# Packing the last 96 columns of gate and up into fewer TensorE matmuls, in a scheduled two-block kernel

## The chip, the core and the metric

The kernel runs on one core of one Trainium2 chip. The metric is device time in microseconds (us) of that core, lower is better. "The profile" is a page and a trace of one execution; times in it count from the start of its span, and the span is about 1.7 us shorter than the device time of the same run. Engines are named as in the profile: PE is TensorE (PEld its weight loads), DVE is VectorE, ACT is ScalarE, POOL is GpSimd, SP is the engine whose queue issues nearly all DMAs here.

## The reference, cut to what matters

Four residual layers in a row: linear attention (A), gated ReGLU (B), A, B, with the same weights both times. S is 2048 tokens, D is 512, H is 32 heads of 16, F is 1376. All data are bfloat16.

```python
x = x + A(layernorm(x))   # qkv, softmax feature maps, kv state, normalise, wo
x = x + B(layernorm(x))
x = x + A(layernorm(x))
x = x + B(layernorm(x))

def B(x, W_gate, W_up, W_down):
    gate = x @ W_gate             # [2048, 512] @ [512, 1376]
    up   = x @ W_up
    return (relu(gate) * up) @ W_down
```

The number that matters is 1376 = 10 x 128 + 96. A full matmul of this kernel has 128 columns of weights (its stationary operand) and N tokens (its moving operand, N = 512 in most of them). The last chunk of gate and the last chunk of up each use 96 of the 128 columns.

## The kernel before

Tokens are 16 tiles of 128, or 4 slabs of 512. For each slab and each chunk `fc` of 128 columns, `step` does four matmuls for gate and four for up (D = 512 is four contractions of 128), a relu on ACT and a product on DVE. The sums of a matmul land in a bank of PSUM, from which ACT and DVE read them:

```python
def step(fc):
    Mf = 128 if fc < 10 else FLAST                       # FLAST = 96
    gb, ub = next(ring), next(ring)                      # two PSUM banks
    ...
    for bank, W, wr in ((gb, k.Wg, "Wg"), (ub, k.Wu, "Wu")):
        for ic in range(NC):                             # NC = 4
            op("pe", ... e.matmul(k.pb[bank][0:Mf, 0:n], W[:, ic, fc*128:fc*128+Mf],
                                  k.yT[:, ic, c0:c0+n], start=(ic == 0), stop=(ic == NC-1)),
               [r(wr, ic)] + RY, [self.RP[bank]], du, ...)
    op("act", ... relu: gate_sb <- pb[gb] ..., 170 + n * 0.833, ...)
    ...                                                  # product on DVE into hT[u]
for fc in range(NFC):                                    # NFC = 11
    out.append(lambda fc=fc: step(fc))
```

The kernel is not written in its final order. Every instruction is recorded as an `op` with what it reads, what it writes, its engine and a fixed duration. At build time a list scheduler works out ranks from the end of the program backwards, simulates it forwards, tries 48 variants of the ranks, and keeps the order with the shortest makespan (the modelled time to the last end, averaged over 6 replays with slightly varied durations). This order of each engine is then what runs.

```python
def _forward(self, prio):
    ...
        nxt[e] = min([(max(free[e], t), prio[i], i) for i, t in avail[e].items() if place[i] < lim], default=None)
    ...
        free[o.eng] = st + o.dur            # an engine is held for the op's fixed duration
        if o.is_dma:
            q_free = max(st + self.DMA_FIXED * 0.35, q_free) + o.dma_bytes / self.DMA_BW
            finish[i] = q_free + self.DMA_FIXED * 0.65
```

The first layer norm applies its scale and shift, mostly on DVE, and each tile is then transposed by a DMA on SP's queue. The late weights (8 pieces of `wo`, gate, up, down) are loaded on the same queue. In the model an ordinary DMA holds SP for 450 ns, a transpose for 1190 ns; a DVE instruction takes the same time whatever GpSimd does.

```python
# ln(): tiles 4 to 15 of the first layer norm
op(how, ... e.tensor_scalar(k.ytile[:, yb, :], k.x_sb[:, t, :], k.rstd[:, t, :], k.nmr[:, t, :], ...),
   dep, dst, 407 if how == "dve" else 2090, f"{tag} apply {t}")
self.dma_tr(... k.yT[:, :, t*128:(t+1)*128] <- k.ytile[:, yb, :] ..., f"{tag} tr {t}")      # "L0 tr 14" below

# late_weights(): on SP as well
dma("sp", ... k.wo_p[h:128:8, :, :] <- wo_v[h] ..., 65536, f"dma wo{h}")                    # h = 0..7
dma("sp", ... W[:, c, :] <- src[c*128:(c+1)*128, :] ..., 128 * F * 2, f"dma {nm}{c}")       # Wg, Wu
```

The softmax here doesn't subtract the row's maximum and nothing guards it: scores larger than these inputs give would overflow.

Of the kernel before, what the change touches and what calls it, by code (L numbers as in the profile page):

```python
# [368 lines left out]
class Kernel:  # L369
# [27 lines left out]
    def alloc(self, E):  # L397
        nc = self.nc

        def sb(name, shape, dt=BF16):  # L400
            t = E(nc.sbuf_tensor(name, [P] + shape, dt))
            setattr(self, name, t)
            return t

        sb("x_sb", [NT, 512])
        sb("yT", [NC, S])
        sb("wv_p", [NC, 512])
        sb("Wqp", [NC, 512])
        sb("Wkp", [NC, 512])
        sb("wo_p", [NC, 512])  # L410
        sb("Wg", [NC, F])
        sb("Wu", [NC, F])
        sb("Wd", [NFC, 512])
        sb("expk", [NT, 2, 512])
        sb("vsb", [NT, NC, 130])
        sb("expq", [NSLAB, NC, 2, 512])
        sb("kvbd", [NG, GW])
        sb("hT", [NHU, 512])
        sb("numbf", [2, NG, GW])
        sb("tsc", [2, 1024])  # L420
        sb("osb", [2, 512])
        sb("oT", [4, NC, 128])
        sb("gate_sb", [3, 512])
        sb("ytile", [4, 512])
        sb("ident", [128])
        sb("mask8", [8])
        sb("mask8t", [8])
        sb("phi_c", [NC, DH])
        sb("stats6", [NT, 6], FP32)
        sb("mv", [NT, 2], FP32)  # L430
        sb("rv1", [NT, 1], FP32)
        sb("rstd", [NT, 1], FP32)
        sb("nmr", [NT, 1], FP32)
        sb("agg", [4, 3], FP32)
        sb("aggw", [2], FP32)
        sb("mhalf", [4, 1], FP32)
        sb("Zk", [2, 64], FP32)
        sb("rZk", [4, 64], FP32)
        sb("zm", [2, 64], FP32)
        sb("zd", [2, 32], FP32)  # L440
        sb("zr", [2, 32], FP32)
        sb("ab", [2, 64])
        self.ps = E(nc.psum_tensor("ps", [P, 8, 512], FP32))
        self.pb = [self.ps[:, i, :] for i in range(8)]
        self.RP = [self.r("pb", i) for i in range(8)]


    def setup(self):
# [17 lines left out]
        op("pool", lambda e: e.affine_select(k.mask8t[:], ones_c[:, 0:8], [[-16, 8]], ALU.is_ge, 0.0, base=0, channel_multiplier=1),  # L466
           [r("tsc", 0)], [r("mask8t")], 200, "mask8 a")
        op("pool", lambda e: e.affine_select(k.mask8[:], k.mask8t[:], [[16, 8]], ALU.is_ge, 0.0, base=15, channel_multiplier=-1),
           [r("mask8t")], [r("mask8")], 200, "mask8 b")

        n0 = len(self.prog.ops)

        def ldx(t0, t1, after=()):
            dma("sp", lambda e: e.dma_start(k.x_sb[:, t0:t1, :], xv[:, t0:t1, :]), list(after), [r("x", t) for t in range(t0, t1)], 131072 * (t1 - t0) if t1 > t0 + 1 else 96000, f"dma x{t0}")
        dma("sp", lambda e: e.dma_start(k.phi_c[:], A_w_phi.rearrange("(kc hl) d f -> (hl d) kc f", hl=8)), [], [r("phi_c")], 16384, "dma phi")
        for ic in range(NC):
# [10 lines left out]
        for j, o in enumerate(self.prog.ops[n0:]):  # L487
# [5 lines left out]
            k.mask8[:].unsqueeze(1).unsqueeze(3).to_broadcast([P, NC, 8, DH]), ALU.mult),  # L493
           [r("phi_c"), r("mask8")], [R_BD], 1040, "BD")
        op("pool", lambda e: e.memset(k.aggw[:, 0:1], -0.5), [], [r("aggw")], 100, "agg w0")
# [246 lines left out]

    def glu_up(self, ts, ring, tag, out, on_act=()):
        op, r, k = self.op, self.r, self
# [27 lines left out]

        for fc in range(NFC):
            out.append(lambda fc=fc: step(fc))

    def glu_down(self, t, ring, tag, halves=1):
# [20 lines left out]
    def emit(self):  # L797
        from itertools import cycle
        self.unit, self.unit_of = 0, {}
        self.setup()  # L800
# [28 lines left out]
        for i, piece in enumerate(pieces):  # L829
            piece(self.r("yT", 15 if i < 8 else 15))  # L830
        kv(6, 2)
        kv(8, 2)
# [6 lines left out]
        for li in (0, 2):  # L839
# [10 lines left out]

            def steps_B(ts, on_act=()):
                out = []
                self.glu_up(ts, gring, B, out, on_act)
                for t in ts:
                    out.append(lambda t=t: self.glu_down(t, dring, B, 1 + (last and t == NT - 1)))
                    if last:
                        out.append(lambda t=t: self.store(t, 1 + (t == NT - 1)))
                return out

            def steps_N(ts):  # L860
                return [lambda t=t: N([t]) for t in ts]
# [29 lines left out]
            if not last:  # L891
                mix(steps_B(tiles(2)), steps_N([14, 15]) + steps_K(0))
                mix(steps_B(tiles(3)), steps_K(1) + steps_K(2) + [lambda: self.q_proj(0, mring, "A2")])
                for t in range(12):
                    self.kv_acc(t, "A2")
                for f in steps_K(3):
                    f()
                for t in tiles(3):
                    self.kv_acc(t, "A2")
                self.kv_fin("A2")  # L900
            else:
                mix(steps_B(tiles(2), HA), [])
                mix(steps_B(tiles(3), HA), [])

# [67 lines left out]
```

## Time and profile before

| | before |
|---|---|
| device time, median of 3 runs | 391.91 us (391.82 to 392.07) |
| span of the profiled run | 390.3 us |
| granted TensorE clock | 1.000 |
| PE busy | 379.4 us, 97% |
| start to start of two N=512 matmuls in a full stretch | 0.216 us |

These are the first line of the page of the kernel before (busy time, share of the span, instructions) and the first line of its chain of waits (which engines make up the chain that ended last).

```profile
PE 379.4 (97%) x2331; PEld 208.0 (53%) x2331; DVE 272.0 (70%) x547; ACT 206.6 (53%) x389; POOL 168.5 (43%) x284
PE 88%; POOL 4%; ACT 3%; DMA 2%; DVE 1%; issue 1%; ACTq 0%; POOLq 0%
```

TensorE bounds it. That is not so over the whole length, as the table of busy time by stretch of the same kernel shows (stretch, its length, then PE, PEld, DVE, ACT, POOL busy us with instruction counts, granted clock, DMA share, GB/s):

```profile
0.00:50.00 50.00, 44.15 (x311) 24.96 (x311) 44.43 (x70) 39.81 (x60) 39.87 (x59) 1.00 0.57 153
...
100.00:150.00 50.00, 50.00 (x271) 24.93 (x270) 37.82 (x80) 18.41 (x36) 22.58 (x49) 1.00 0.24 43
```

The two largest PE waits before (who waited, for what: total us, times, longest):

```profile
PE ps L509 <- DMA hT<-in_A_wqkv_dram: 3.6, 2, 3.2
PE ps L617 <- ACT yT L605: 1.0, 1, 1.0
```

The groups by shape of the same kernel show what the change is after (line, engine, operation, out<-in, stationary, moving, count | busy us, mean ns | idle before). A matmul is drawn 379 ns long but its successor starts after 216 ns; these 0.216 us are called a slot below.

```profile
L758 PE MATMUL ps<-yT,Wu 128*96 128x512 bf16 x24 | 9.1, 379 | 0.0
L758 PE MATMUL ps<-yT,Wg 128*96 128x512 bf16 x24 | 8.9, 379 | 0.0
```

There are 24 and 24 of these matmuls, each using 96 of 128 columns (slabs 1 to 3 of both gated layers, four contractions each; the missing slab 0 runs in halves of N=256).

### The profile page before, as it was taken

Reading aid. Unit: us, or ns where it says so; the run is one execution under the profiler, and the core shown is the slowest. Engines: PE = TensorE matmul, PEld = TensorE weight load, DVE = VectorE, ACT = ScalarE, POOL = GpSimd, SP = SyncE. Lnnn points to the kernel's source line nnn. Section 1 sums busy time; section 2 is a strip of 40 time slices with the busy share of each in tenths; the row PEclk is TensorE's granted clock in tenths of the full one; section 3 lists DMA queues with packets and bytes.
Section 4 is the critical chain, followed back from the end, with each engine's and each line's share of the span. In section 5 each row is a group of like instructions: output and inputs, shape, how many; then the busy total and the mean of one; then the engine's idle time right before and its main releaser. Section 6 shows DMA issues by size and latency. Waiting matters only on the chain.

```text
span 390.3 us, 6397 instructions
## 1 busy us (share of the span) xinstructions
PE 379.4 (97%) x2331; PEld 208.0 (53%) x2331; DVE 272.0 (70%) x547; ACT 206.6 (53%) x389; POOL 168.5 (43%) x284
## 2 busy tenths in 40 slices
PE   5999989999999999999999999999999999999997
PEld 3445554667644544444444457567774554444444
DVE  4999978877766888866766777897986776232222
ACT  5898859834633404533453484985563462553340
POOL 5499936641724363372244543584553242100000
DMA  6833682311311322401000110132323132100002
GB/s 179 228 67 71 191 299 53 69 40 32 53 40 27 43 55 44 84 10 28 14 15 0 27 29 3 40 80 57 55 55 69 27 42 67 29 14 27 17 12 67
DMA packets 61663, 23.01 MB, mean 59 GB/s; under 512 B 53472, under 2 KB 60608, under 8 KB 61632
## 3 DMA queue, kind: packets, MB, share of 16 engines
q1 hardware_dynamic: 60912, 22.02, 24.4%
q10 hardware_dynamic: 720, 0.59, 0.5%
q8 instruction: 18, 0.29, 0.3%
q14 instruction: 13, 0.11, 0.1%
HBM read 7.91 MB, written 2.10 MB: 26 GB/s over the span
## 4 chain that ended last, share of the span: by engine, by line
PE 88%; POOL 4%; ACT 3%; DMA 2%; DVE 1%; issue 1%; ACTq 0%; POOLq 0%
PE ps L758 39%; PE ps L785 19%; PE ps L617 7%; PE ps L737 7%; PE ps L690 6%; PE ps L706 4%; PE ps L663 3%; PE ps L648 2%; POOL expk L634 2%; ACT expq L693 2%; DVE stats L551 1%; DMA x_sb<-in_A_x_dram 1%; DMA hT<-in_A_wqkv_dram 1%; ACT expk L620 1%; POOL rstd L576 1%
## 5 line engine op out<-in xcount | busy, mean ns | idle before, releaser
L758 PE MATMUL ps<-yT,Wg 128*128 128x512 bf16 (+3 forms) x440 | 130.1, 337 | 0.5 <-DMA yT<-ytile 0.2
L758 PE MATMUL ps<-yT,Wu 128*128 128x512 bf16 (+3 forms) x440 | 129.6, 336 | 0.0
L760 ACT ACTIVATE gate_sb<-ps 128x512 bf16<-128x512 f32 (+3 forms) x110 | 55.9, 512 | 105.3 <-PE ps L758 102.9
L785 PE MATMUL ps<-Wd,hT 128*128 128x512 bf16 (+2 forms) x363 | 106.8, 373 | 0.0
L634 POOL TENSOR_TENSOR expk<-expk,rZk 128x1024 bf16<-128x1024 bf16 (+1 forms) x32 | 59.5, 1878 | 37.1 <-DVE rZk L631 19.7
L758 PEld LDWEIGHTS ps<-yT,Wg 128*128 128x128 bf16 (+1 forms) x440 | 43.4, 100 | 33.8 <-issue 1.1
L758 PEld LDWEIGHTS ps<-yT,Wu 128*128 128x128 bf16 (+1 forms) x440 | 43.7, 100 | 32.6 <-ACT expk L765 0.2
L767 DVE TENSOR_TENSOR hT<-gate_sb,expk 128x512 bf16<-128x512 bf16 (+3 forms) x73 | 29.8, 409 | 37.9 <-ACT expk L765 33.0
L785 PEld LDWEIGHTS ps<-Wd,hT 128*128 128x128 bf16 (+1 forms) x363 | 35.3, 98 | 36.6 <-DVE x_sb L787 0.6
L551 DVE BATCH_NORM_STATS2 stats<-x_sb 128x6 f32<-128x512 bf16 x64 | 42.6, 682 | 5.5 <-DMA x_sb<-in_A_x_dram 5.1
L366 ACT ACTIVATE numbf<-ps 128x432 bf16<-128x432 f32 x64 | 33.1, 536 | 19.5 <-PE ps L706 19.4
L629 DVE TENSOR_REDUCE Zk<-expk 128x64 f32<-128x1024 bf16 x32 | 37.7, 1194 | 5.7 <-ACT expk L620 5.4
L731 POOL TENSOR_TENSOR osb<-tsc 128x512 bf16<-128x512 bf16 x28 | 32.5, 1162 | 19.9 <-DVE tsc L726 17.8
L737 PE MATMUL ps<-wo_p,oT 128*128 128x512 bf16 x128 | 39.8, 379 | 0.0
L770 DVE TENSOR_TENSOR hT<-gate_sb,ps 128x512 bf16<-128x512 bf16 (+2 forms) x37 | 22.7, 613 | 20.8 <-PE ps L758 19.6
L693 ACT ACTIVATE expq<-ps 128x1024 bf16<-128x1024 f32 (+1 forms) x40 | 32.6, 861 | 7.3 <-PE ps L690 7.0
L765 ACT ACTIVATE expk<-ps 128x512 bf16<-128x512 f32 (+3 forms) x73 | 36.1, 497 | 0.1
L706 PE MATMUL ps<-kvbd,expq 128*128 128x144 bf16 x256 | 35.0, 226 | 0.5 <-ACT numbf L366 0.5
L620 ACT ACTIVATE expk<-ps 128x512 bf16<-128x512 f32 x44 | 23.9, 598 | 21.5 <-PE ps L617 21.2
L690 PE MATMUL ps<-yT,Wqp 128*128 128x512 bf16 x128 | 34.6, 379 | 0.6 <-ACT expq L693 0.5
L787 DVE TENSOR_TENSOR x_sb<-x_sb,ps 128x512 bf16<-128x512 bf16 (+1 forms) x33 | 22.0, 669 | 18.8 <-PE ps L785 18.4
L559 POOL TENSOR_TENSOR rstd<-rv,mhalf 128x1 f32<-128x1 f32 (+1 forms) x53 | 31.9, 607 | 2.9
(73 smaller groups left out, 429.2 us busy)
## 6 DMA issues: line engine op xcount, KB each, us to landing
out_dram<-x_sb SPq DMA_DIRECT2D x15, 128.0 KB, 1.7
x_sb<-in_A_x_dram SPq DMA_DIRECT2D x3, 512.0 KB, 6.2
Wu<-in_B_W_up_dram SPq DMA_DIRECT2D x4, 344.0 KB, 5.9
Wg<-in_B_W_gate_dram SPq DMA_DIRECT2D x4, 344.0 KB, 5.5
Wd<-in_B_W_down_dram SPq DMA_DIRECT2D x5, 256.0 KB, 6.9
yT<-ytile SPq DMA_TRANSPOSE x60, 2.5
hT<-in_A_wqkv_dram ACTq DMA_DIRECT2D x4, 128.0 KB, 3.1
x_sb<-in_A_x_dram SPq DMA_DIRECT2D x4, 128.0 KB, 3.7
```

The source lines that it names most:

```text
L366: return e.activation(out, in_, ACT.Copy) if hasattr(e, "activation") else e.tensor_copy(out, in_)
L551: op("dve", (lambda t: lambda e: e.bn_stats(k.stats6[:, t, :], k.x_sb[:, t, :]))(t), [r("x", t)], [r("st", t)], 685, f"{tag} stats {t}")
L629: op("dve", lambda e: e.tensor_reduce(k.Zk[:, zb, :], k.expk[:, t, :, :].rearrange("p s (h f) -> p (s h) f", f=16), AX.X, ALU.add), [r("ex ...
L634: op(eng, (lambda s0, s1: lambda e: e.tensor_tensor(k.expk[:, t, s0:s1, :].rearrange("p s (h f) -> p (s h) f", f=16), k.expk[:, t, s0:s1, ...
L690: op("pe", (lambda c, ic, bank: lambda e: e.matmul(k.pb[bank][:], k.Wqp[:, ic, c * 128:(c + 1) * 128], k.yT[:, ic, st * 512:(st + 1) * 512 ...
L693: op("act", (lambda c0, s, b0: lambda e: e.activation(k.expq[:, st, c0:c0 + w, s, :], k.ps[:, b0:b0 + w, :], ACT.Exp, scale=(1.0 - 2.0 * s ...
L706: op("pe", (lambda s, c, j, g0, bank: lambda e: e.matmul(k.pb[bank][:, j * GW:(j + 1) * GW], k.expq[:, st, c, s, tt * 128:(tt + 1) * 128], ...
L737: op("pe", (lambda c, bank: lambda e: e.matmul(k.pb[bank][:], k.oT[:, ob, c, :], k.wo_p[:, c, :], start=(c == 0), stop=(c == NC - 1)))(c, ...
L758: op("pe", (lambda bank, W, ic, fc, Mf: lambda e: e.matmul(k.pb[bank][0:Mf, 0:n], W[:, ic, fc * 128:fc * 128 + Mf], k.yT[:, ic, c0:c0 + n] ...
L760: op("act", (lambda Mf, gb, gs: lambda e: e.activation(k.gate_sb[0:Mf, gs, 0:n], k.pb[gb][0:Mf, 0:n], ACT.Relu))(Mf, gb, gs), [self.RP[gb] ...
L765: op("act", (lambda Mf, ub, tu: lambda e: e.activation(k.expk[0:Mf, tu, 0, 0:n], k.pb[ub][0:Mf, 0:n], ACT.Copy))(Mf, ub, tu), [self.RP[ub] ...
L785: op("pe", (lambda fc, Kf, u, c0, bank, m0, m1: lambda e: e.matmul(k.pb[bank][:, m0:m1], k.hT[0:Kf, u, c0:c0 + 128], k.Wd[0:Kf, fc, m0:m1] ...
```

## The change

In the last two slabs of each gated layer the remaining 96 columns of gate and 96 of up are split. 64 + 64 of them form one full 128-column stationary, one group of four matmuls per slab. The remaining 32 + 32 form a 64-column stationary, which is meant to be used on both halves of the array's columns at once, one half for slab 2 and one for slab 3: eight matmuls that are hoped to take four slots. Per layer, 16 slots for two slabs become 8 + 4. GpSimd copies the columns once into a packed weight tile `Wr`, 192 columns wide. To make room, two small setup tensors move into buffers that are free at that time.

The diff, cut to its core (the rest are the buffer moves and the bookkeeping of which buffer of `hT` belongs to which slab):

```diff
+        sb("Wr", [NC, 192])
-        sb("mask8t", [8])
-        sb("phi_c", [NC, DH])
+        self.mask8t = self.tsc[:, 1, 0:8]
+        self.phi_c = self.hT[:, 13, 0:NC * DH].rearrange("p (c f) -> p c f", c=NC)
...
+    def pack_weights(self):
+        for W, nm, o0, o1 in ((k.Wu, "Wu", 0, 128), (k.Wg, "Wg", 64, 160)):
+            for dst, src, n in ((o0, 1280, 64), (o1, 1344, 32)):
+                op("pool", ... e.tensor_copy(k.Wr[:, :, dst:dst + n], W[:, :, src:src + n]) ..., 200 + 4 * n, f"pack {nm} {dst}")
...
-        for fc in range(NFC):
+        def short64():
+            ...
+            for ic in range(NC):
+                op("pe", ... e.matmul(k.pb[bank][:, 0:n], k.Wr[:, ic, 0:128], k.yT[:, ic, c0:c0 + n], ...), ..., du, ...)
+            op("act", ... relu: gate_sb[0:64] <- pb[bank][64:128] ...)
+            op("dve", ... hT[0:64] <- gate_sb[0:64] * pb[bank][0:64] ...)
+
+        def short32():
+            ...
+            def mm(e):
+                for ic in range(NC):
+                    for v in range(2):
+                        last = e.matmul(k.pb[bank][v * 64:v * 64 + 64, 0:n], k.Wr[:, ic, 128:192], k.yT[:, ic, c0 + v * n:c0 + v * n + n], start=(ic == 0), stop=(ic == NC - 1), skip_group_check=True)
+                return last
+            op("pe", mm, ..., 4 * du + 190, ...)
+            ...                                   # relu and product of 32 partitions, once per slab
+
+        for fc in range(NFC - 1 if short else NFC):
             out.append(lambda fc=fc: step(fc))
+        if short:
+            out.append(short64)
+        if short == 2:
+            out.append(short32)
...
-                mix(steps_B(tiles(2)), steps_N([14, 15]) + steps_K(0))
-                mix(steps_B(tiles(3)), steps_K(1) + steps_K(2) + ...)
+                mix(steps_B(tiles(2), (), 2), steps_N([14, 15]) + steps_K(0))
+                mix(steps_B(tiles(3), (), 1), steps_K(1) + steps_K(2) + ...)
...
-                mix(steps_B(tiles(2), HA), [])
-                mix(steps_B(tiles(3), HA), [])
+                mix(steps_B(tiles(2), HA, 2), [])
+                mix(steps_B(tiles(3), HA, 1), [])
```

The diff fixes no instruction's place in the running order: as before, the scheduler orders everything anew.

More of the change, by code (lines that the diff above doesn't have):

```diff
@@ L466, in setup @@
         op("pool", lambda e: e.affine_select(k.mask8t[:], ones_c[:, 0:8], [[-16, 8]], ALU.is_ge, 0.0, base=0, channel_multiplier=1),
-           [r("tsc", 0)], [r("mask8t")], 200, "mask8 a")
+           [r("tsc", 0)], [r("tsc", 1)], 200, "mask8 a")
         op("pool", lambda e: e.affine_select(k.mask8[:], k.mask8t[:], [[16, 8]], ALU.is_ge, 0.0, base=15, channel_multiplier=-1),
-           [r("mask8t")], [r("mask8")], 200, "mask8 b")
+           [r("tsc", 1)], [r("mask8")], 200, "mask8 b")
         n0 = len(self.prog.ops)
@@ L474, in ldx @@
             dma("sp", lambda e: e.dma_start(k.x_sb[:, t0:t1, :], xv[:, t0:t1, :]), list(after), [r("x", t) for t in range(t0, t1)], 131072 * (t1 - t0) if t1 > t0 + 1 else 96000, f"dma x{t0}")
-        dma("sp", lambda e: e.dma_start(k.phi_c[:], A_w_phi.rearrange("(kc hl) d f -> (hl d) kc f", hl=8)), [], [r("phi_c")], 16384, "dma phi")
+        dma("sp", lambda e: e.dma_start(k.phi_c[:], A_w_phi.rearrange("(kc hl) d f -> (hl d) kc f", hl=8)), [], [r("hT", 13)], 16384, "dma phi")
         for ic in range(NC):
@@ L493, in setup @@
             k.mask8[:].unsqueeze(1).unsqueeze(3).to_broadcast([P, NC, 8, DH]), ALU.mult),
-           [r("phi_c"), r("mask8")], [R_BD], 1040, "BD")
+           [r("hT", 13), r("mask8")], [R_BD], 1040, "BD")
         op("pool", lambda e: e.memset(k.aggw[:, 0:1], -0.5), [], [r("aggw")], 100, "agg w0")
@@ L740, in num, with glu_up @@
            [r("x", t), self.RP[bank]], [r("x", t)], 685, f"{tag} resid {t}")
-    def glu_up(self, ts, ring, tag, out, on_act=()):
+    def pack_weights(self):
+        op, r, k = self.op, self.r, self
+        for W, nm, o0, o1 in ((k.Wu, "Wu", 0, 128), (k.Wg, "Wg", 64, 160)):
+            for dst, src, n in ((o0, 1280, 64), (o1, 1344, 32)):
+                op("pool", (lambda W, dst, src, n: lambda e: e.tensor_copy(k.Wr[:, :, dst:dst + n], W[:, :, src:src + n]))(W, dst, src, n),
+                   [r(nm, ic) for ic in range(NC)], [r("Wr", dst)], 200 + 4 * n, f"pack {nm} {dst}")
+    def glu_up(self, ts, ring, tag, out, on_act=(), short=0):
         op, r, k = self.op, self.r, self
@@ L771, in step @@
                    [r("gate", gs), self.RP[ub]], [r("hT", u)], 150 + n * 1.04, f"{tag} h {ts[0]} {fc}")
-        for fc in range(NFC):
-            out.append(lambda fc=fc: step(fc))
+        def short64():
+            bank = next(ring)
+            u = self.short_of.pop(ts[0], None)
+            if u is None:
+                u = self.new_short(ts)
+            gs = u % 3
+            for ic in range(NC):
+                op("pe", (lambda ic: lambda e: e.matmul(k.pb[bank][:, 0:n], k.Wr[:, ic, 0:128], k.yT[:, ic, c0:c0 + n], start=(ic == 0), stop=(ic == NC - 1)))(ic),
+                   [r("Wr", 0), r("Wr", 64)] + RY, [self.RP[bank]], du, f"{tag} Wr {ts[0]} {ic}")
+            op("act", lambda e: e.activation(k.gate_sb[0:64, gs, 0:n], k.pb[bank][64:128, 0:n], ACT.Relu),
+               [self.RP[bank]], [r("gate", gs)], 170 + n * 0.833, f"{tag} relu {ts[0]} a")
+            op("dve", lambda e: e.tensor_tensor(k.hT[0:64, u, 0:n], k.gate_sb[0:64, gs, 0:n], k.pb[bank][0:64, 0:n], ALU.mult),
+               [r("gate", gs), self.RP[bank]], [r("hT", u)], 150 + n * 1.04, f"{tag} h {ts[0]} a")
@@ new lines, in short32 @@
+        def short32():
+            bank = next(ring)
+            t2 = list(range(ts[-1] + 1, ts[-1] + 1 + len(ts)))
+            us = [self.unit_of[ts[0], NFC - 1][0], self.new_short(t2)]
+            self.short_of[t2[0]] = us[1]
+            def mm(e):
[3 more added lines that the diff above has]
+                return last
+            op("pe", mm, [r("Wr", 128), r("Wr", 160)] + RY + [r("yT", t) for t in t2], [self.RP[bank]], 4 * du + 190, f"{tag} Wr2 {ts[0]}")
+            for v, u in enumerate(us):
+                gs = u % 3
+                op("act", (lambda v, gs: lambda e: e.activation(k.gate_sb[64:96, gs, 0:n], k.pb[bank][v * 64 + 32:v * 64 + 64, 0:n], ACT.Relu))(v, gs),
+                   [self.RP[bank]], [r("gate", gs)], 170 + n * 0.833, f"{tag} relu {ts[0]} b{v}")
+                op("dve", (lambda v, gs, u: lambda e: e.tensor_tensor(k.hT[64:96, u, 0:n], k.gate_sb[64:96, gs, 0:n], k.pb[bank][v * 64:v * 64 + 32, 0:n], ALU.mult))(v, gs, u),
+                   [r("gate", gs), self.RP[bank]], [r("hT", u)], 150 + n * 1.04, f"{tag} h {ts[0]} b{v}")
@@ L776, in glu_down, with new_short @@
+        for fc in range(NFC - 1 if short else NFC):
+            out.append(lambda fc=fc: step(fc))
+        if short:
+            out.append(short64)
+        if short == 2:
+            out.append(short32)
+    def new_short(self, ts):
+        u = self.unit % NHU
+        self.unit += 1
+        for t in ts:
+            self.unit_of[t, NFC - 1] = (u, (t - ts[0]) * 128)
+        return u
     def glu_down(self, t, ring, tag, halves=1):
@@ L798, in emit @@
         from itertools import cycle
-        self.unit, self.unit_of = 0, {}
+        self.unit, self.unit_of, self.short_of = 0, {}, {}
         self.setup()
@@ L830, in emit @@
             piece(self.r("yT", 15 if i < 8 else 15))
+        self.pack_weights()
         kv(6, 2)
@@ L849, in N, with steps_B @@
                     self.ln(t, L1)
-            def steps_B(ts, on_act=()):
+            def steps_B(ts, on_act=(), short=0):
                 out = []
-                self.glu_up(ts, gring, B, out, on_act)
+                self.glu_up(ts, gring, B, out, on_act, short)
                 for t in ts:
@@ L891, in emit @@
             if not last:
-                mix(steps_B(tiles(2)), steps_N([14, 15]) + steps_K(0))
-                mix(steps_B(tiles(3)), steps_K(1) + steps_K(2) + [lambda: self.q_proj(0, mring, "A2")])
+                mix(steps_B(tiles(2), (), 2), steps_N([14, 15]) + steps_K(0))
+                mix(steps_B(tiles(3), (), 1), steps_K(1) + steps_K(2) + [lambda: self.q_proj(0, mring, "A2")])
                 for t in range(12):
```

## The prediction

> **What bounds the kernel now.** TensorE. The page has PE busy for 379.4 of 390.3 us (97%). That figure overstates the matmul work, because a 128x512 matmul is drawn 379 ns long while the timeline shows the next one starting 216 ns later. But the busy-time table by stretch gives 50.00 of 50 us from 100 to 200 us and 49.8 from 200 to 300, and the waits view lists no PE wait over 0.2 us in the gated layers. From about 70 us on, PE starts a matmul every 216 ns (N=512) without a hole. The chain of waits agrees: 88% PE, 39% in the gate/up line. So a 216 ns matmul slot taken away in the gated layers should come off the span almost one for one.
>
> **What the change removes.** The last 96 columns of gate and up take 4+4 matmuls of N=512 per slab. The view by shape lists them: 128x96 stationary, 24 for each weight over slabs 1 to 3 of both layers. In slabs 2 and 3 of a layer that is 16 slots = 16 x 0.216 = 3.46 us. After: two packed groups of 4 full-width matmuls (8 slots, 1.73 us), and one group of 8 matmuls on 64-column halves. If halves run in pairs those 8 cost 4 slots, 0.86 us. Ideal gain: 4 slots = 0.86 us per layer, 1.73 us in all.
>
> **What eats into it.** (a) [...] My estimate of one drain is the part of a matmul the timeline overlaps, 379 - 216 = 163 ns. Once or twice per group: 0.16 to 0.33 us per layer. [...] Expected net gain: 0.5 to 0.7 us per layer, about 1.2 us in all.
>
> **What it adds elsewhere.** Two relus and two multiplies more per layer (32 partitions, same free size: 0.59 us on ACT, 0.68 us on DVE each, by the shapes before); ACT is 53% busy and DVE 70%, neither in the chain there. In the last layer, slabs 2 and 3 lose an ACT copy. Four weight copies on POOL, some 2 us in all (estimated from the 128x512 add at 1.15 us); the gate and up loads land around 53 us and the POOL timeline is idle from 52.0 to 60.1 us, so they fit. Short group of slab 2 needs slab 3's transposes; these come early. All orders are recomputed by the list scheduler, which can move the kernel by some tenths of a microsecond either way, at the layer boundaries (40 to 72 us and 235 to 260 us, where PE has its small waits).
>
> **Prediction.** 390.7 us (391.9 - 1.2), range 389.6 to 392.0. Faster by over 2%: 0.01; within 2%: 0.98; slower by over 2%: 0.01.
>
> **What the profile would show.** Right: 32 fewer 128x96 matmuls, 16 full-width packed ones and 16 on halves; the halves start in pairs a few ns apart, pairs about 216 ns apart; a hole of 0.1 to 0.3 us around each group; PE still without holes elsewhere; span 1.0 to 1.5 us shorter. Wrong: halves starting 216 ns apart (no pairing: the gain is zero or a small loss); weight loads on the halves no longer hidden; POOL copies delaying the k normalisation before 60 us.
>
> **What would make it wrong.** Serialised halves; drains far longer than 163 ns; or a new order that opens a wait near 50 or 245 us, or, better than thought, closes one.

"Drain" stands for time lost at the edges of that group, with a size estimated from 379 and 216 ns. The sum came to 0.5 to 0.7 us per layer, about 1.2 us in all. It is what the first term alone leaves of the ideal gain: 0.86 us less 0.16 to 0.33 us is 0.53 to 0.70 us.

## More of the kernel before

From 100 to 200 us PE has no hole, and from 200 to 300 us only 0.4 us of them. In the first 50 us it has some 6 us of them, with DVE as busy as PE.

## The result, and the profile after

| | before | after |
|---|---|---|
| device time, median of 6 runs | 391.87 us (391.16 to 392.07) | 393.66 us (393.24 to 394.04) |
| span of the profiled run | 390.3 us | 391.7 us |
| ratio after/before | | 1.0049, 95% interval 1.0036 to 1.0061 |

Ratios here and below are the mean time of one kernel's runs over that of the kernel before in the same rounds, so they are not quite the ratio of the medians quoted. The change stays within 2%, but the kernel is 1.8 us slower, where 1.2 us faster was predicted. The measured median lies outside the predicted range.

**The packed groups do what they should.** Groups by shape, after:

```profile
L767 PE MATMUL ps<-yT,Wg 128*96 128x512 bf16 x8 | 2.9, 379 | 0.0
L767 PE MATMUL ps<-yT,Wu 128*96 128x512 bf16 x8 | 3.0, 379 | 0.1
L790 PE MATMUL ps<-yT,Wr 128*128 128x512 bf16 x16 | 5.9, 379 | 0.1
L807 PE MATMUL ps<-yT,Wr 128*64 128x512 bf16 x16 | 2.1, 385 | 0.0
```

The 32 narrow matmuls are gone, 16 full packed ones and 16 on halves have come. The order in time of PE around the first group on halves, after (start us, length us, line, instructions):

```profile
165.48 0.81 PE L618 MATMUL ps<-Wkp,yT 128*128 128x512 bf16 x3
166.22 1.05 PE L807 MATMUL ps<-yT,Wr 128*64 128x512 bf16 x8
167.21 0.60 PE L767 MATMUL ps<-yT,Wg 128*128 128x512 bf16 x2
```

Three matmuls start at 165.48, so the slot after them would be at 165.48 + 3 x 0.216 = 166.13. The next ordinary matmul starts at 167.21. The group therefore takes 1.08 us: four slots are 0.86 us, and both edges together cost 0.22 us. The single records start 2, 5, 242, 245, 458, 461, 674 and 677 ns after the group opens: pairs 3 ns apart, then 216 ns to the next pair but for the first step. In slots, a layer now spends 8 x 0.216 + 1.08 = 2.81 us where it spent 16 x 0.216 = 3.46 us. That is 0.65 us less per layer and 1.3 us less in all, close to the 1.2 us predicted.

**The idle time grew by more.** The page of the kernel after, the same two lines as before:

```profile
PE 375.1 (96%) x2290; PEld 205.4 (52%) x2331; DVE 270.7 (69%) x551; ACT 208.3 (53%) x391; POOL 169.9 (43%) x288
PE 81%; DVE 7%; issue 4%; DMA 3%; POOL 2%; ACT 2%; SPq 0%; DVEq 0%; POOLq 0%
```

Part of the fall of PE busy time is not real: 2290 matmul records stand against 2331 weight loads, so 41 are missing from this trace. All 2331 weight loads are recorded in both. So I reckoned idle time from them: the interval between consecutive loads less the nominal slot of the matmul between, summed by stretch. (E1 and E10 are experiments below.)

| TensorE idle, us | before | after | E1 | E10 |
|---|---|---|---|---|
| 0 to 20 | 3.65 | 3.50 | 4.08 | 4.88 |
| 20 to 35 | 0.72 | 2.05 | 0.43 | 0.31 |
| 35 to 55 | 1.13 | 2.00 | 1.35 | 1.27 |
| 55 to 75 | 1.86 | 1.47 | 1.11 | 1.10 |
| 235 to 262 | 1.00 | 0.73 | 1.70 | 0.74 |
| 262 to 300 | 0.26 | 0.64 | 0.10 | 0.09 |
| 300 to 330 | -0.03 | 0.54 | 0.52 | 0.20 |
| whole span | 8.56 | 11.24 | 9.45 | 8.72 |

About 1.3 us of slots went, 2.68 us of idle time came: together +1.4 us, and the spans differ by 391.7 - 390.3 = 1.4 us. (A slightly negative value only means that the nominal slots are a little too long there.) Most of the new idle time lies between 20 and 55 us, more than 100 us before the first packed matmul at 163.3 us. (The first 20 us, which wait for the first loads, differ by up to 1.4 us from run to run and say nothing.)

The PE waits after (compare the two lines of before above):

```profile
PE ps L510 <- DMA hT<-in_A_wqkv_dram: 4.5, 2, 3.3
PE ps L649 <- DMA yT<-ytile: 1.9, 2, 1.5
PE ps L618 <- DMA yT<-ytile: 1.8, 1, 1.8
```

The two `yT<-ytile` waits are new: PE waits for transposed tiles of the first layer norm. Take the later one first, where PE waits, after:

```profile
44.26 1.03 PE L691 MATMUL ps<-yT,Wqp 128*128 128x512 bf16 x4
47.10 0.82 PE L618 MATMUL ps<-Wkp,yT 128*128 128x512 bf16 x3 [1.81 <-DMA yT<-ytile]
```

The queue of SP in the order of time shows why. Before, then after:

```profile
36.03 2.41 SPq L537 DMA_DIRECT2D wo_p<-in_A_wo_dram  x3
38.48 1.27 SPq L597 DMA_TRANSPOSE yT<-ytile  x1
39.80 3.14 SPq L537 DMA_DIRECT2D wo_p<-in_A_wo_dram  x5
```

```profile
36.36 6.07 SPq L538 DMA_DIRECT2D wo_p<-in_A_wo_dram  x8
42.47 0.63 SPq L541 DMA_DIRECT2D Wg<-in_B_W_gate_dram  x1
43.15 0.42 SPq L541 DMA_DIRECT2D Wu<-in_B_W_up_dram  x1
43.61 1.23 SPq L598 DMA_TRANSPOSE yT<-ytile  x1
```

The transpose of tile 14 stood behind three weight loads, at 38.48 us. Now it stands behind ten, at 43.61 us. A `wo` load holds the queue for 6.07/8 = 0.76 us, where the scheduler counts 0.45 us, so it thinks ten loads cheaper by about 2.5 us than they are. The count of bytes does not set this time: a `wo` load has 64 KB, and the two large loads behind, of 344 KB each, held the queue for 0.63 and 0.42 us. The transfer itself took longer too: from issue to landing 2.5 us before and 3.4 us after, by the landing records of the two traces.

The earlier wait, 1.52 us at 25.79 us, begins on DVE. The layer-norm apply of tile 6 next to the product of GpSimd, before and then after (DVE and POOL in the order of time):

```profile
19.62 0.40 DVE L592 TENSOR_SCALAR ytile<-x_sb,rstd,nmr 128x512 bf16<-128x512 bf16 x1
21.07 1.93 POOL L634 TENSOR_TENSOR expk<-expk,rZk 128x1024 bf16<-128x1024 bf16 x1
```

```profile
21.21 1.93 POOL L635 TENSOR_TENSOR expk<-expk,rZk 128x1024 bf16<-128x1024 bf16 x1
21.32 1.96 DVE L593 TENSOR_SCALAR ytile<-x_sb,rstd,nmr 128x512 bf16<-128x512 bf16 x1
```

Before, the apply ran ahead of the GpSimd instruction and took 0.40 us. After, it came 0.11 us behind its start and took 1.96 us, until 0.14 us after its end. This pattern is called "held" below; what in the hardware makes it is not shown. In the kernel after, the timeline has seven applies that start while one of GpSimd's products of large tiles (L635, L732) runs. They took 1.02 to 1.96 us and ended 0.14 to 0.16 us after it. Beside a small GpSimd instruction (128x1, L560) applies still took 0.40 to 0.41 us. Not every DVE instruction is held in this trace. Products of gate with a PSUM bank took 690 ns at most, and statistics and sums, which read SBUF (where the kernel keeps its tiles), kept to 632 to 695 and 1153 to 1222 ns. Held are applies (308 to 1964 ns) and products of two tiles in SBUF (227 to 1045 ns over all sizes). The scheduler's model has 407 ns for an apply always.

The same costs PE time near the end. GpSimd, DVE and PE in the order of time, after:

```profile
320.97 1.15 POOL L732 TENSOR_TENSOR osb<-tsc 128x512 bf16<-128x512 bf16 x1
321.14 1.14 DVE L595 TENSOR_SCALAR ytile<-x_sb,mv,rstd 128x512 bf16<-128x512 bf16 x1 [0.56 <-POOL rstd L560]
322.20 0.52 DVE L776 TENSOR_TENSOR hT<-gate_sb,expk 96x512 bf16<-96x512 bf16 x1
322.77 0.39 PE L840 MATMUL ps<-Wd,hT 96*128 96x512 bf16 x1 [0.39 <-DVE hT L776]
```

An apply is held, the product behind it comes late, and the last down matmul of a tile waits for it: 0.56 us of idle time by the reckoning above.

None of these instructions belongs to the packing. The theory to test, called A in the expectations, is therefore that the packing gains about what was predicted and the new order at the start loses more. Its rival is that the packed groups, or their relus, products and weight copies, cost the time themselves. Where an expectation uses other letters or a number behind A, it says there in words what that theory holds.

### The profile page after: what moved, and what is told of

Same layout as the page of the kernel before. It is cut to its first block, busy times and chain, and to the rows that moved or that the text cites. A ratio compares the mean times of both kernels' runs of the same rounds, so it can differ in the third digit from the quotient of the medians.

```text
span 391.7 us, 6354 instructions
## 1 busy us (share of the span) xinstructions
PE 375.1 (96%) x2290; PEld 205.4 (52%) x2331; DVE 270.7 (69%) x551; ACT 208.3 (53%) x391; POOL 169.9 (43%) x288
## 4 chain that ended last, share of the span: by engine, by line
PE 81%; DVE 7%; issue 4%; DMA 3%; POOL 2%; ACT 2%; SPq 0%; DVEq 0%; POOLq 0%
PE ps L767 36%; PE ps L840 19%; PE ps L618 8%; PE ps L691 6%; PE ps L738 6%; PE ps L707 4%; PE ps L664 2%; DVE stats L552 2%; ACT expq L694 2%; DMA yT<-ytile 2%; DVE Zk L630 1%; DVE rZk L632 1%; POOL rstd L560 1%; DVE ytile L593 1%; DMA x_sb<-in_A_x_dram 1%
## 5 line engine op out<-in xcount | busy, mean ns | idle before, releaser
L767 PE MATMUL ps<-yT,Wu 128*128 128x512 bf16 (+3 forms) x419 | 117.3, 334 | 0.5 <-DVE zr L722 0.2
L767 PE MATMUL ps<-yT,Wg 128*128 128x512 bf16 (+3 forms) x415 | 114.9, 334 | 1.2 <-DMA oT<-osb 0.6
L769 ACT ACTIVATE gate_sb<-ps 128x512 bf16<-128x512 f32 (+3 forms) x106 | 53.0, 509 | 102.6 <-PE ps L767 89.7
L840 PE MATMUL ps<-Wd,hT 128*128 128x512 bf16 (+3 forms) x355 | 104.4, 373 | 0.9 <-DVE hT L776 0.4
L635 POOL TENSOR_TENSOR expk<-expk,rZk 128x1024 bf16<-128x1024 bf16 (+1 forms) x32 | 59.4, 1872 | 37.1 <-DVE rZk L632 28.0
L767 PEld LDWEIGHTS ps<-yT,Wu 128*128 128x128 bf16 (+1 forms) x424 | 42.0, 99 | 31.9 <-ACT expk L774 0.4
L767 PEld LDWEIGHTS ps<-yT,Wg 128*128 128x128 bf16 (+1 forms) x424 | 41.4, 99 | 32.0 <-issue 1.0
L776 DVE TENSOR_TENSOR hT<-gate_sb,expk 128x512 bf16<-128x512 bf16 (+3 forms) x71 | 28.0, 398 | 26.0 <-ACT expk L774 23.5
L732 POOL TENSOR_TENSOR osb<-tsc 128x512 bf16<-128x512 bf16 x28 | 32.7, 1166 | 18.6 <-DVE tsc L727 15.5
L738 PE MATMUL ps<-wo_p,oT 128*128 128x512 bf16 x123 | 38.6, 379 | 0.2
L559 POOL TENSOR_SCALAR rv<-mv 128x1 f32<-128x1 f32 (+1 forms) x53 | 13.3, 260 | 49.5 <-DVE mv L554 49.3
L560 POOL TENSOR_TENSOR rstd<-rv,mhalf 128x1 f32<-128x1 f32 (+1 forms) x53 | 30.9, 587 | 2.6
L618 PE MATMUL ps<-Wkp,yT 128*128 128x512 bf16 x85 | 28.1, 379 | 2.9 <-DMA yT<-ytile 1.8
```

The source lines that it names most:

```text
L618: op("pe", (lambda ic, bank, W: lambda e: e.matmul(k.pb[bank][:], k.yT[:, ic, t * 128:(t + 1) * 128], W[:, ic, :], start=(ic == 0), stop=( ...
L635: op(eng, (lambda s0, s1: lambda e: e.tensor_tensor(k.expk[:, t, s0:s1, :].rearrange("p s (h f) -> p (s h) f", f=16), k.expk[:, t, s0:s1, ...
L738: op("pe", (lambda c, bank: lambda e: e.matmul(k.pb[bank][:], k.oT[:, ob, c, :], k.wo_p[:, c, :], start=(c == 0), stop=(c == NC - 1)))(c, ...
L767: op("pe", (lambda bank, W, ic, fc, Mf: lambda e: e.matmul(k.pb[bank][0:Mf, 0:n], W[:, ic, fc * 128:fc * 128 + Mf], k.yT[:, ic, c0:c0 + n] ...
L769: op("act", (lambda Mf, gb, gs: lambda e: e.activation(k.gate_sb[0:Mf, gs, 0:n], k.pb[gb][0:Mf, 0:n], ACT.Relu))(Mf, gb, gs), [self.RP[gb] ...
L840: op("pe", (lambda fc, Kf, u, c0, bank, m0, m1: lambda e: e.matmul(k.pb[bank][:, m0:m1], k.hT[0:Kf, u, c0:c0 + 128], k.Wd[0:Kf, fc, m0:m1] ...
```

## The experiments

All experiments ran with several rounds beside the kernel before on the same chip. The fixed orders are imposed after the scheduler has run: a function takes given per-engine sequences, or moves one instruction ahead of or behind another, and rebuilds the start times. All dependencies and semaphores are derived afterwards as usual. Clocks below 0.999 are given where they occur.

### E1: packing, with the start of before

The start of each engine's order, 568 instructions in all and roughly the first 52 us, is put in the order of the kernel before. The rest stays as in the kernel after.

```diff
+FIRST = {"sp": "dma phi|dma x0|...|L0 tr 15|dma wo0|dma wo1|dma wo2|L0 tr 14|dma wo3|...", "act": ..., "pe": ..., "dve": ..., "pool": ...}
 prog.schedule()
+prog.impose(first=FIRST)
```

> The changed kernel, with the instructions that the kernel before ran in its first 52 us put back into the order they had there on every engine; the rest in the order of the changed kernel. Theory A (the packing itself gains 1.3 us of TensorE time, and the loss comes from the new order at the start): about 391.3 us, 391.0 to 391.6, and the two TensorE waits of 1.5 and 1.8 us for transposed tiles before 50 us are gone. Rival B (the packed and halved matmuls or their extra evictions cost the time where they run, after 160 us): stays at 393.7 us.

Measured: 391.28 us (390.36 to 392.15), before on the same chip 392.08 us; ratio 0.9974, interval 0.9956 to 0.9992. Against before the kernel after stood at 1.0049, so the start alone is worth 0.75%, or 2.9 us. With the old start the packed kernel is faster than before, if by only 0.8 us. This supports theory A and speaks against its rival: all packed groups, relus, products and copies are still there. Both waits of 1.5 and 1.8 us for tiles are gone (one of 0.4 us for a tile is left). Two waits of PE in E1 that lie after the start:

```profile
PE ps L825 <- DMA oT<-osb: 1.0, 1, 1.0
PE ps L898 <- DVE hT L834: 0.4, 1, 0.4
```

So the order of the later layers keeps two holes, at 261.8 us and 320.7 us, that the kernel before did not have at this size. E10 returns to them.

### E2: no packing, with the start of after

The reverse: the kernel before, with its start in the order of the kernel after.

```diff
+FIRST = {"sp": "dma phi|...|L0 tr 15|L0 tr 12|dma wo0|dma wo1|...", ...}     # order of the kernel after
 prog.schedule()
+prog.impose(first=FIRST)
```

> The kernel before, without any packing, with only the first 49 us of instructions in the order of the changed kernel. Theory A: the loss of the start comes without the packing, about 393.9 us, 393.3 to 394.5, with TensorE waits for transposed tiles of about 3.5 us before 50 us. Rival B: stays at 391.9 us.

Measured: 396.31 us (395.35 to 396.87), ratio 1.0105, interval 1.0088 to 1.0121. The direction is that of theory A: a kernel without any packing loses time by this order alone. The size is not: 4.2 us against its before. PE in the order of time at tile 14:

```profile
46.65 1.14 PE L675 MATMUL ps<-Wkp,yT 128*128 128x512 bf16 x3 [2.15 <-DMA yT<-ytile]
48.97 0.63 PE L675 MATMUL ps<-wv_p,yT 128*128 128x512 bf16 x1
```

The wait is 2.15 us, and a matmul behind it is drawn 0.63 us long instead of 0.38. The table of busy time by stretch shows why: the granted clock behind the wait was 0.50 in E2 and 1.00 in the kernel after (E2 first, then the kernel after):

```profile
48.00:50.00 2.00, 1.99 (x10) 1.17 (x10) 0.63 (x1) 1.58 (x3) 1.35 (x1) 0.50 1.00 373
48.00:50.00 2.00, 2.00 (x18) 1.28 (x18) 0.71 (x1) 1.59 (x4) 2.00 (x2) 1.00 1.01 328
```

In steps of 1 us the clock of E2 from 47 to 51 us is 0.51, 0.50, 0.50 and 0.78, so 1.7 us of full-speed time were lost there, which is what a mean clock of 0.996 over the whole run amounts to. The profiled run (395.35 us) is 3.3 us over before; less these 1.7 us, 1.6 us are left, near the 1.9 us expected. Four of five runs have this clock. But the fifth has 1.000 and took 396.27 us all the same; it has no trace, and what it lost stays open.

### E3: the kernel after, with one DVE instruction moved ahead

The apply of tile 6 goes back in front of the reciprocal of the first k tile, and so ahead of the GpSimd product.

```diff
 prog.schedule()
+prog.impose(moves=[("L0 apply 6", "before", "A0 rZk 0")])
```

> The changed kernel with one VectorE instruction moved: the normalisation of tile 6 goes ahead of the reciprocal and the sum of tiles 0 and 1, as it stood before. Theory A1 (it is held by the GpSimd multiply that runs beside it, 1.96 us for an instruction that takes 0.31 us alone, and all later transposes queue behind it): it takes about 0.4 us, the TensorE wait of 1.5 us at 25.8 us is gone, and the time is 392.2 to 393.2 us, since the second wait at 47 us stays. Rival A2 (only the late transposes of tile 14 bound the start): 393.7 us, no change, the first wait gone and given back at 47 us.

Measured: 394.62 us (393.77 to 395.95), ratio 1.0064, interval 1.0045 to 1.0084. No gain over the kernel after. The move itself worked. DVE, then PE at tile 14, in the order of time of E3:

```profile
20.79 0.40 DVE L643 TENSOR_SCALAR ytile<-x_sb,rstd,nmr 128x512 bf16<-128x512 bf16 x1
```

```profile
48.04 0.82 PE L668 MATMUL ps<-Wkp,yT 128*128 128x512 bf16 x3 [2.55 <-DMA yT<-ytile]
49.52 0.63 PE L668 MATMUL ps<-wv_p,yT 128*128 128x512 bf16 x1
```

The apply takes 0.40 us and the wait of 1.52 us near 26 us has gone (0.3 and 0.4 us in two smaller waits are left). But the wait for tile 14 grew to 2.55 us. PE came there at 45.49 us (45.29 in the kernel after). The transpose was issued at 43.75 us (43.61), but PE could go on only at 48.04 us (47.10), so this transfer took longer; why is not shown. PE did not even come earlier, since it had idled some 0.9 us more in the first 20 us of this run. The total agrees with rival A2: as long as the tile comes late, nothing is gained ahead of it. The two runs with a granted clock of 1.000 took 393.77 and 393.88 us, the four at 0.995 to 0.996 took 394.28 to 395.95 us. In the profiled one of those the clock behind the wait is again 0.50, from 50 to 52 us.

### E4: the kernel after, with one DMA moved ahead

The transpose of tile 14 goes ahead of the last two `wo` loads and the two large loads.

```diff
 prog.schedule()
+prog.impose(moves=[("L0 tr 14", "after", "dma wo5")])
```

> The changed kernel with one DMA issue moved: the transpose of tile 14 goes ahead of four weight loads in the queue, after the sixth of the eight small ones. Theory A2 (the transpose stood 2.8 us behind loads nobody needed yet): it is issued at about 41 us in place of 43.6, the TensorE wait of 1.8 us at 47 us is gone, the time 391.9 to 392.7 us. Rival A1 (the loss was made before, at tile 6): gain under 0.5 us, 393.2 us or more.

Measured: 392.24 us (391.47 to 393.00), ratio 1.0001, interval 0.9986 to 1.0016. SP's queue in the order of time, E4:

```profile
36.70 4.70 SPq L588 DMA_DIRECT2D wo_p<-in_A_wo_dram  x6
41.44 1.27 SPq L648 DMA_TRANSPOSE yT<-ytile  x1
```

The transpose is issued at 41.44 us instead of 43.61. The wait for tile 14 is no longer in the list of waits; the earlier wait, for the apply, remains at 1.1 us. One DMA moved by four places recovers 1.0049 - 1.0001 = 0.48%, about 1.9 us. E3 and E4 together say which of the two new waits binds: the later one.

### E5: the eight matmuls on halves in serial order

Is the pairing a matter of how the eight matmuls are written? E5 exchanges the loops, so that four of one half come first and then four of the other.

```diff
-                for ic in range(NC):
-                    for v in range(2):
+                for v in range(2):
+                    for ic in range(NC):
```

> The changed kernel with the two nested loops of the halved group exchanged: all four matmuls of the first half, then all four of the second, so that neighbours are on the same half. Nothing else moves, the instruction order is the same. Theory A (neighbours on different halves run side by side, 8 matmuls in 1.08 us): the group takes about 1.73 us plus its edges, 0.6 to 0.9 us more in each gated layer, and the time is 1.2 to 1.8 us over the changed kernel's 393.7 us. Rival C (the group was short for another reason, such as the narrower stationary): no change.

Measured: 394.84 us (393.10 to 395.98), ratio 1.0066, interval 1.0043 to 1.0089. The total seems to say that serial order costs 1.2 us against the kernel after. The group says that it costs nothing. PE in the order of time, E5:

```profile
167.56 0.81 PE L618 MATMUL ps<-Wkp,yT 128*128 128x512 bf16 x3
168.31 1.06 PE L807 MATMUL ps<-yT,Wr 128*64 128x512 bf16 x8
169.30 0.60 PE L767 MATMUL ps<-yT,Wg 128*128 128x512 bf16 x2
```

From 167.56 + 3 x 0.216 = 168.21 to 169.30 it is 1.09 us, as before. The records start at 2, 15, 242, 255, 458, 471, 674 and 687 ns: still pairs. So the idea that only program neighbours pair is wrong. Eight on one half took 1.85 us (E11), so matmuls of the second half must have started here before earlier ones of the first had. This is inferred, since a record does not tell the half, and the serial order on one half was not run. The extra time is at the start: the order is the same as in the kernel after, but the wait for tile 14 was 2.1 us in this profile, a matmul behind it was again drawn 0.63 us, and idle time from 35 to 55 us came to 3.80 us instead of 2.00. Of this, 1.7 us are again a stretch at half clock (0.88, 0.50, 0.50, 0.50 and 0.91 in steps of 1 us from 47 us), which the reckoning counts as idle time. The two runs with a clock of 0.996 took 395.47 and 395.98 us, the four at 1.000 between 393.10 and 394.98 us. How far a start with this order loses thus varies from one run to the next, and a total says little about one group. The group has to be read by itself.

### E9: the kernel before, with one DMA moved back

Does the place of that one transpose suffice without any other part of the new order? E9 is the kernel before with the transpose of tile 14 in the place that it has in the kernel after, behind eight `wo` and two large loads (issued at 43.05 us in its trace).

```diff
 prog.schedule()
+prog.impose(moves=[("L0 tr 14", "after", "dma Wg2")])
```

> The kernel before, with one DMA issue moved and nothing else: the transpose of tile 14 goes behind five more small weight loads and two large ones in the queue, where the changed kernel has it. Theory A2 (this one place in the queue is what the new order loses at): it is issued at 42 to 43 us in place of 38.5, TensorE waits 3 to 4.5 us for the tile at about 41.6 us, and the time is 394.5 to 396.5 us. Rival (the rest of the new order at the start matters more): under 393 us.

Measured: 399.96 us (399.39 to 400.39), ratio 1.0200, interval 1.0182 to 1.0218. One DMA in the queue makes 8 us. The granted clock was 0.991 in three of the four runs and 0.996 in one. The wait and PE behind it in the order of time, E9:

```profile
PE ps L667 <- DMA yT<-ytile: 6.1, 1, 6.1
```

```profile
47.68 3.60 PE L667 MATMUL ps<-Wkp,yT 128*128 128x512 bf16 x8 [6.14 <-DMA yT<-ytile]
```

The same eight in the kernel before:

```profile
41.62 1.89 PE L617 MATMUL ps<-Wkp,yT 128*128 128x512 bf16 x8
```

The row of the clock, E9:

```profile
PEclk9999889999999999999999999999999999999999
```

The wait is 6.1 us, and the cost does not end with it. Eight matmuls take 3.60 us where the same eight took 1.89 us in the kernel before, about half speed, and the clock row (40 slices of 10 us) dips in the two slices from 40 to 60 us. In steps of 1 us the clock is 0.50 from 47 to 53 us and lies between 0.50 and 1.00 in the step on either side: 3.4 us of full-speed time lost. The 6.1 us of wait and these 3.4 us, less the 1.1 us that the kernel before idles from 35 to 55 us anyway, come to 8.4 us; the spans differ by 398.5 - 390.3 = 8.2 us. Waits of 2.15, 2.55 and 2.10 us at the same place were also followed by a clock of 0.50, in the profiled runs of E2, E3 and E5, while the one of 1.81 us in the kernel after was not (clocks 0.999 to 1.000 in all its runs). In these traces, then, the four waits of over 2 us for tile 14 cost more than their length. What sets the clock, and from what wait on, is not shown. The expectation was missed on the large side. The wait is longer than in the kernel after although the transpose is issued 0.6 us earlier. The larger reason is that PE's order is that of before and wants tile 14 at 41.5 us, while the kernel after puts other matmuls first, until 45.3 us. Besides, PE went on 4.6 us after the issue here and 3.5 us after it there, so the transfer took longer; why is not shown. So a place in the queue has no fixed price: the same place costs what the consumer's order makes of it.

### E7 and E8: a scheduler told what the trace shows

If the scheduler is blind to the queue and to the holds of DVE, tell it. In E7 (packed) and E8 (not packed) a `wo` load holds SP for 760 ns, a large load for 560 ns, and a DVE instruction of the kinds seen held (applies, products of two tiles in SBUF) that meets a GpSimd instruction ends after that one.

```diff
+        for o in ops:
+            if o.is_dma and o.name.startswith("dma wo"):
+                o.dur = 760.0
+            elif o.is_dma and o.name.startswith("dma W"):
+                o.dur = 560.0
+            o.port = o.eng == "dve" and (" apply " in o.name or " phik " in o.name or o.name in copied)
...
+    def _held(self, o, t, pool_end, f=1.0):
+        if o.port and pool_end - 170.0 > t:
+            return max(o.dur * f, pool_end + 140.0 - t)
+        return o.dur * f
```

> The changed kernel, with the scheduler told two costs that the traces show and its model lacked: a weight load costs 0.76 or 0.56 us in the DMA queue in place of 0.45, and a VectorE instruction of the kinds that were seen held (normalisation, product of two tiles in SBUF) ends no earlier than the GpSimd instruction beside it. It orders the first 60 us the same way with and without the packing. Theory A: the transpose of tile 14 is issued early, no wait for it, the hole of 0.56 us at 322.8 us goes; 390 to 391.5 us, under the kernel before. Rival B: the packed kernel stays over 393 us.

> The kernel before, under the same better informed scheduler. With the one above it is a pair with nearly the same order on both sides. Theory A: 1.0 to 1.6 us slower than the packed one of this pair (1.29 us of TensorE time), so 391.2 to 392.8 us. Rival B (packing costs time where it runs): equal to or faster than the packed one.

Measured: E7 393.35 us (393.16 to 393.90), ratio 1.0036, interval 1.0020 to 1.0051. E8 395.32 us (394.58 to 395.53), ratio 1.0079, interval 1.0061 to 1.0097. E7 did not come out faster than before, so this expectation was missed, and by its letter the level is the rival's (over 393 us). E8 missed its level too, by more than 2 us. The hole of E7 near 322 us has gone (idle from 300 to 330 us is -0.02 us), but from 35 to 75 us it idles 5.2 us, before 3.0 us. The largest single piece is a wait of 1.27 us for a transposed tile that was issued at 35.39 us and landed 4.0 us later, where the median of all 60 is 2.4 us. Why the rest of the better informed start is worse stays open; other costs are still missing from the model. The pair still tells one thing, against rival B: the packed kernel is the faster one of the two. Their idle totals are the same, 11.18 and 11.25 us, so here is a comparison in which the schedules are about equally good: the spans differ by 392.8 - 391.4 = 1.4 us and the medians by 2.0 us in favour of packing. That agrees with the 1.3 us of slots.

### E10: E1 with two instructions moved

The two holes left in E1 have one instruction each at their head. An output-projection matmul waits for a transposed attention tile at 261.8 us, and a down matmul waits for the late product at 320.7 us. Both go some places back in PE's order.

```diff
-prog.impose(first=FIRST)
+prog.impose(first=FIRST, moves=[("A2 wo 5 0", "after", "B3 Wu 0 4 3"), ("B3 down 4 10", "after", "B3 Wg 8 0 2")])
```

> The changed kernel with the old start, as in the first experiment, and two matmuls moved later on TensorE: the one that waited 0.94 us at 261.8 us for a transposed tile of the attention layer goes 16 matmuls of 256 back, and the one that waited 0.55 us at 320.7 us for a gated product goes two matmuls back. Theory A (what is left to lose after the old start are these two holes): up to 1.4 us less than the 391.28 us of the first experiment, 390.0 to 390.8 us, ratio to the kernel before 0.993 to 0.996. Rival: the waits only move to the next matmul that needs the same thing, and it stays at 391.3 us.

Measured: 390.11 us (389.24 to 390.67), before on the same chip 391.77 us; ratio 0.9955, interval 0.9943 to 0.9967. This beats both kernels, the one before by 1.7 us. The comparison with the reference passed (E11 shows how little that says). The waits for `oT` and `hT` are gone from the list, and the table of idle time above shows it: from 235 to 262 us 1.70 became 0.74, from 300 to 330 us 0.52 became 0.20. The whole idle time is 8.72 us, that of before 8.56 us. So with idle time of the same size, 1.3 us fewer slots make a span of 388.9 instead of 390.3 us. Since idle time is reckoned from the span, this says only that the idle time did not grow; whether a slot counts for its full length is tested by E11. The two moves were made by hand in this kernel alone, so E10 is no comparison of equally tuned orders, but one of orders with equal idle time.

### E11: both slabs on the same half

Is it the two halves that pair, or is a 64-column stationary quicker in itself? E11 is E1 with both slabs written to the same half of the bank. The sums of both slabs go to the same place, so the result is wrong, while instructions and amounts stay the same. (The comparison with the reference passed it all the same; 32 of 1376 columns in half the slabs are evidently within its tolerance. A passed comparison thus does not vouch for the halved group in the other runs either.)

```diff
-  last = e.matmul(k.pb[bank][v * 64:v * 64 + 64, 0:n], k.Wr[:, ic, 128:192], ...)
+  last = e.matmul(k.pb[bank][0:64, 0:n], k.Wr[:, ic, 128:192], ...)
   ... relu and product of both slabs read partitions 32:64 and 0:32
```

> The old start again, but both slabs of the halved group are computed on the same 64 columns, one over the other (wrong result on purpose: the second slab's last 32 columns overwrite the first's). Width of the stationary, number of matmuls, order, evictions and their sizes stay. Theory D (the halves are two queues that fill side by side whatever the program order): the 8 matmuls now start 216 ns apart, the group takes 1.7 to 2.0 us in place of 1.08, and the time is 1.3 to 1.8 us over the first experiment's 391.28. Rival C (a 64-column stationary is enough to be quick): 1.08 us and 391.3 us as before.

Measured: 392.67 us (392.39 to 393.19), ratio 1.0028, interval 1.0015 to 1.0041; E1 had 0.9974, so this is 0.54% or 2.1 us more by the ratios, and 1.4 us by the medians. PE in the order of time, E11:

```profile
163.50 1.91 PE L865 MATMUL ps<-yT,Wr 128*64 128x512 bf16 x8
165.35 0.60 PE L825 MATMUL ps<-yT,Wg 128*128 128x512 bf16 x2
```

Eight matmuls on one half take 165.35 - 163.50 = 1.85 us, eight on two halves 167.21 - 166.22 = 0.99 us by the same reading. A narrow stationary alone saves nothing. The two halves do. (That they are "two queues" is the wording of theory D; the records show starts only.) E11 also tests the price of a slot: its order is that of E1, its two groups take 2 x 0.86 = 1.7 us longer on PE, and the run is 1.4 to 2.1 us longer.

### Built but not timed

Orders at build time show where the new start comes from. With only the weight copies and the buffer moves, or only the latter, the start keeps the order of before. With the packed groups in only one of the two gated layers, whichever, it changes. So groups from 163 us on reorder instructions whose first difference, on DVE, is modelled at 5.6 us. That fits a scheduler that ranks from the end backwards. By its own model the change was a gain, 391.70 to 390.49 us: right about the slots, blind to the costs at the start.

## Why the prediction was wrong, and where it was right

- **"TensorE" bounds the kernel, and a slot taken away "should come off the span almost one for one".** Right for the slots: E11 is 1.4 to 2.1 us longer than E1 for 1.7 us more of slots. E10, with idle time as before, is 1.4 us shorter in span than before for 1.3 us fewer slots, and E7 against E8 gives the same 1.4 us.
- **Pairing, drains and 64 + 64: "about 1.2 us in all".** Right. The group on halves took 1.08 us. Both edges together cost 0.22 us, within the 0.16 to 0.33 us that the prediction estimated from 379 and 216 ns; whether it is a drain that costs them is not shown. Pairing lost nothing in the group beyond that (0.216 us from pair to pair). The saving came to 1.3 us.
- **Relus, products and weight copies harmless.** Right. The copies took 0.29 to 0.40 us each from 54.2 us on, right behind POOL's last product and with no other POOL work until 60 us, some 1.4 us in all instead of 2, and with all of these in it E1 is faster than before.
- **The step that failed:** "All orders are recomputed by the list scheduler, which can move the kernel by some tenths of a microsecond either way, at the layer boundaries (40 to 72 us and 235 to 260 us, where PE has its small waits)." The term was mis-sized and partly misplaced. It measured +2.7 us of TensorE idle time, twice the gain, of which 1.3 us came at 20 to 35 us, 0.9 at 35 to 55 and 0.6 at 300 to 330. The second of these lies in the stretch named; the other two do not, and the boundary at 235 to 262 us did not lose. E1 shows that the start order decides (2.9 us by ratios). E4 shows that one DMA's place is 1.9 us of it. E3 shows that the larger hold on DVE, removed by itself, gains nothing.
- **"a new order that opens a wait near 50 or 245 us"** was named as what would make it wrong. The wait at 47 us is that one. But the range, 389.6 to 392.0, left 1.3 us above the forecast for this and all other losses together, and nearly as much below it, as if the order were noise about zero. The kernel before was a tuned one, so its order was likely a good draw among those that the model cannot tell apart, and a new draw was more likely to be slower.
- **"PE still without holes elsewhere; span 1.0 to 1.5 us shorter"**: wrong for the kernel after (holes at 26, 47, 264 and 323 us, span 1.4 us longer), true of the span in E10.

That the order of before was a lucky or tuned draw is argued from the results, not shown. Not settled are the run of E2 at full clock, why transposes issued behind large loads took 3.4 to 4.6 us to land instead of 2.5, and why E7's better informed model made a start that still idles.

## What to carry to other kernels

When a build-time scheduler orders the program, a change that saves 1 us at the end can reorder the start: compare the two orders before costing anything, and fix the parts that the change does not touch. A small gain can be measured honestly only with the rest of the order held equal; E1 and E10 gave it, the plain change did not. Where two waits follow one another on the bounding engine, try the later one first: here curing the earlier one alone (E3) gained nothing, curing the later one (E4) gained 1.9 us. Where a wait on TensorE is long, read the granted clock behind it too: in E2, E3, E5 and E9 half clock added 1.7 to 3.4 us behind waits of 2.1 to 6.1 us.
